# Turning q and k of the last batch with transposing transfers between SBUF copies instead of TensorE, under a newly laid order of steps

## The chip, the cores and the metric

The kernel runs on one core of a Trainium2 chip. The metric is the device time of one execution in microseconds (us); smaller is better. The core has a matrix engine (TensorE, PE in the rows), VectorE (DVE), ScalarE (ACT), GpSimd (POOL), and SyncE (SP), which here only issues transfers. Each engine works through its own instructions strictly in the order in which they were issued to it, so an instruction that waits holds up all that stands behind it on that engine.

## The reference

Two layers, one after the other. First attention over 4 batches, 8 heads, 768 positions and 64 values per head: heads 0, 2 and 6 are "retrieval" heads with a full causal mask, the other five are "streaming" heads that see 4 sink positions and a window of 64.

```python
scores = scale * np.matmul(q, k.transpose(0, 1, 3, 2))
scores = np.where(mask, scores, -1e9)
a = np.exp(scores - max); a = a / a.sum(-1)
x = np.matmul(a, v)            # [4, 8, 768, 64] -> x: [4, 768, 512]
```

Then a mixing layer on x:

```python
theta = x @ w_theta
zr, zi = x * np.cos(theta), x * np.sin(theta)
y = w_tok_r @ zr + w_tok_i @ zi          # over the 768 positions
u = x + y
out = u + np.maximum(u @ w_ch, 0.0)
```

## The kernel before, in words

Everything is cut into 128-row tiles: 6 position tiles per batch, 4 pairs of heads per batch ("n" 0 to 3), and per batch 17 units of scores, each a piece of the causal triangle or band for one pair of heads. The whole program is one list of short steps, the string ORDER (line 53), written out by hand or by a planner. Lines 469 to 510 walk through the list and call one small function per step. So the list fixes the order on every engine and every transfer queue; the semaphores between engines come from the data. A step's name tells what it does: the first number is the batch, the last a PSUM bank or the engine (D for VectorE, A for ScalarE, P for GpSimd).

The steps that matter here, for one batch b:

- `lq` (load_qk, line 226): GpSimd issues the load of q or k of one pair into qb or kb, cast to bf16. Position p*6+j lies on partition p, block j. In batch 0 `lf` and `cf` do this with SyncE loads and casts.
- `tq` (turn_qk, line 249): TensorE transposes that pair, 12 transposes of 64 columns for b > 0 (line 255), into a PSUM bank. `eq` (keep_qk, line 259 on ScalarE, 261 on VectorE) copies the bank to qT or kT and puts the positions into their order on the way (strided). `ko` builds shifted keys for streaming heads.
- `s` (score, line 299), `e` (exp on ScalarE, line 326/329), `m` (mask on VectorE, lines 339 to 351), `av` (values, line 386, TensorE), `n` (norm, lines 391 and 393, VectorE) give x.
- `xd` (line 398) turns a tile of x with a SyncE transposing transfer into xT; in batch 0 `xp`/`xe` do it with TensorE. `th` (theta, line 422), `tc`/`ts` (cosine and sine on ScalarE, 425/428), `z` (the products, line 433, on VectorE or GpSimd).
- `mx` (mix, line 441, four 512-column matmuls), `u` (add, 453), `ud` (SyncE transposing transfer of u, 398), `ch` (channel, 457), `o` (finish, 460), `st` (SyncE store, 463).
- `lt`, `wt`, `we` load and turn the token weights once; `lv`, `cv`, `bv`, `sv` load and cast v; `lw` loads w_theta and w_ch; `pw` (spare, line 467) issues 0 to 5 matmuls whose result nobody reads.

The batches are interleaved: while batch b's scores and exponentials run, TensorE fills the gaps with `mx` and `ch` of batch b-1. The buffers that matter: one qb and one kb for all batches, one qT and kT for each pair, 8 PSUM banks, 4 output tiles, 6 u tiles.

The eight turns of batch 3 stand in the list of before like this: six `tq` together after the last scores of batch 2, two later, after the second theta of batch 2 (line numbers 84, 85 and 89).

Of the kernel before, what the change touches and what calls it, by code (L numbers as in the profile page):

```python
# [56 lines left out]
s.0.12.5 ko.0.2.P tq.0.k.1.1 cf.q.1.P k.2 eq.0.k.1.1.D e.0.12.5 cf.k.3.P s.0.15.3 e.0.15.3 s.0.1.5 m.0.0 s.0.7.1 lv.0.2 ko.0.1.D lt.2.0 e.0.1.5
tq.0.k.3.0 lv.0.4 lq.1.q.0 pw.11.1.4 m.0.15 cv.0.0.D s.0.6.3 pw.17.0.7 tq.0.q.1.5 m.0.2 lq.1.k.1 sv.0.D e.0.7.1 cf.q.3.P e.0.6.3 k.vt s.0.10.6
eq.0.k.3.0.A e.0.10.6 eq.0.q.1.5.D pw.16.3.1 lt.1.0 s.0.3.2 e.0.3.2 tq.0.q.3.1 ko.0.3.P m.0.1 lv.0.5 s.0.4.4 m.0.12 s.0.14.6 lq.1.k.3 eq.0.q.3.1.D
e.0.4.4 tq.1.q.0.3 m.0.7 s.0.8.1 m.0.6 eq.1.q.0.3.D wt.2.0.4 e.0.14.6 cv.0.3.P lv.1.0 m.0.3 s.0.5.5 bv.0.0.A lq.1.k.2 pw.9.3.7 e.0.8.1 s.0.9.6 m.0.4  # L60
e.0.5.5 m.0.8 e.0.9.6 we.2.0.4.D s.0.16.2 bv.0.3.P lw.t s.0.13.0 m.0.5 cv.0.1.A m.0.9 av.0.0.4 e.0.13.0 n.0.0.4 av.0.1.6 bv.0.1.P e.0.16.2 cv.0.2.P
tq.1.k.3.1 eq.1.k.3.1.A lq.1.q.1 wt.1.0.0 we.1.0.0.A cv.0.4.A n.0.1.6 bv.0.2.P lt.2.1 m.0.16 av.0.2.2 n.0.2.2 xp.0.1.5 pw.10.0.7 tq.1.k.1.6 tq.1.k.2.7
av.0.3.0 m.0.13 xe.0.1.5.A bv.0.4.D av.0.4.2 lq.1.k.0 cv.0.5.D eq.1.k.1.6.A lt.1.1 n.0.3.0 xp.0.0.4 xe.0.0.4.A lt.0.1 av.0.5.5 lq.1.q.3 n.0.4.2 lv.1.2
xp.0.2.0 xp.0.3.1 k.half eq.1.k.2.7.A xp.0.4.4 lt.3.1 xe.0.3.1.D xe.0.2.0.A th.0.0.2 xe.0.4.4.D ko.1.3.P n.0.5.5 xp.0.5.4 ko.1.1.D ko.1.2.P xe.0.5.4.D
lt.0.0 at.0.S tc.0.0.2 lq.1.q.2 th.0.1.6 ts.0.0.2 z.0.0.r.0.D tq.1.q.1.4 eq.1.q.1.4.D z.0.0.r.1.P tc.0.1.6 lv.1.3 th.0.2.1 z.0.0.i.0.D ts.0.1.6 lv.1.1
wt.1.1.3 wt.2.1.0 z.0.0.i.1.D we.1.1.3.D we.2.1.0.D wt.0.1.6 tc.0.2.1 z.0.1.i.1.P tq.1.k.0.4 tq.1.q.3.5 ts.0.2.1 we.0.1.6.D mx.0.2.0.3 z.0.2.r.1.P
eq.1.q.3.5.D s.1.13.6 z.0.2.i.0.P s.1.8.1 at.4.E eq.1.k.0.4.D wt.3.1.5 we.3.1.5.D e.1.8.1 mx.0.1.0.0 lt.3.0 lq.2.q.3 wt.0.0.4 z.0.2.r.0.D z.0.2.i.1.D
e.1.13.6 tq.1.q.2.5 cv.1.0.A s.1.9.1 e.1.9.1 we.0.0.4.D s.1.1.6 e.1.1.6 eq.1.q.2.5.D z.0.1.i.0.D mx.0.1.2.0 z.0.1.r.1.P lv.1.4 lt.5.1 mx.0.2.2.3
s.1.15.4 lq.2.k.2 s.1.2.1 e.1.2.1 z.0.1.r.0.D s.1.12.6 sv.1.D e.1.15.4 mx.0.1.1.0 u.0.1.0 lq.2.k.3 mx.0.2.1.3 m.1.15 cv.1.3.P lv.1.5 lq.2.k.1 s.1.4.1
lt.5.0 e.1.12.6 bv.1.3.P u.0.2.3 lq.2.k.0 lt.4.0 e.1.4.1 s.1.0.4 s.1.16.6 m.1.8 mx.0.0.1.0 wt.3.0.3 mx.0.0.0.0 e.1.16.6 e.1.0.4 we.3.0.3.D lq.2.q.2  # L70
ud.0.2 s.1.7.1 s.1.5.7 s.1.3.3 e.1.7.1 m.1.9 m.1.16 lw.c m.1.1 s.1.6.5 e.1.6.5 mx.0.0.2.0 e.1.3.3 cv.1.2.P m.1.4 u.0.0.0 m.1.6 cv.1.1.D mx.0.3.1.2
s.1.11.5 m.1.0 s.1.14.0 m.1.7 e.1.5.7 tq.2.k.3.3 e.1.14.0 m.1.3 tq.2.q.3.7 wt.5.0.4 we.5.0.4.D mx.0.3.0.2 e.1.11.5 m.1.5 eq.2.q.3.7.A bv.1.1.P
mx.0.3.2.2 lt.4.1 m.1.2 bv.1.0.P eq.2.k.3.3.A wt.5.1.6 u.0.3.2 av.1.2.0 bv.1.2.A we.5.1.6.D av.1.1.4 s.1.10.6 e.1.10.6 tq.2.k.2.2 tq.2.k.0.3 n.1.2.0
m.1.13 tq.2.k.1.1 tq.2.q.2.0 eq.2.q.2.0.A mx.0.5.1.7 n.1.1.4 cv.1.4.P bv.1.4.P eq.2.k.1.1.D xd.1.1 av.1.0.5 mx.0.5.2.7 eq.2.k.2.2.A ko.2.2.P n.1.0.5
mx.0.5.0.7 xd.1.0 ko.2.3.P wt.4.1.6 av.1.3.1 cv.1.5.P m.1.12 we.4.1.6.A av.1.4.4 xd.1.2 n.1.3.1 lq.2.q.1 ch.0.2.6 wt.4.0.2 n.1.4.4 lq.2.q.0 av.1.5.0
xd.1.3 at.1.S xd.1.4 th.1.0.4 we.4.0.2.D n.1.5.0 u.0.5.7 xd.1.5 ud.0.1 eq.2.k.0.3.D th.1.1.0 tc.1.0.4 o.0.2.6 ts.1.0.4 lv.2.4 s.2.7.2 tc.1.1.0
tq.2.q.1.6 ud.0.3 tq.2.q.0.5 z.1.0.i.1.P ts.1.1.0 st.0.2 mx.0.4.2.7 z.1.0.i.0.D ud.0.0 z.1.1.r.1.D ch.0.1.4 eq.2.q.1.6.A lv.2.1 th.1.2.0 ko.2.1.D
z.1.0.r.1.D lv.2.0 ch.0.3.6 z.1.0.r.0.D z.1.1.i.1.D mx.0.4.1.7 z.1.1.r.0.D o.0.1.4 ts.1.2.0 z.1.2.i.1.D tc.1.2.0 lv.2.3 ud.0.5 mx.0.4.0.7 z.1.1.i.0.P
o.0.3.6 mx.1.1.0.0 z.1.2.r.0.P u.0.4.7 z.1.2.i.0.D ch.0.0.1 e.2.7.2 ud.0.4 lq.3.q.1 eq.2.q.0.5.A o.0.0.1 mx.1.3.1.7 s.2.9.3 s.2.12.5 lq.3.q.0 lq.3.q.2
lq.3.q.3 e.2.9.3 cv.2.4.P s.2.4.1 mx.1.3.0.7 e.2.12.5 z.1.2.r.1.D mx.1.3.2.7 lq.3.k.1 s.2.5.5 m.2.12 s.2.2.3 cv.2.3.A bv.2.3.A lq.3.k.3 cv.2.0.D  # L80
bv.2.0.P u.1.3.7 ch.0.5.6 e.2.2.3 e.2.4.1 e.2.5.5 st.0.1 o.0.5.6 cv.2.1.P mx.1.1.1.0 lq.3.k.2 st.0.5 s.2.13.3 s.2.15.1 s.2.14.6 m.2.9 sv.2.P e.2.15.1
mx.1.1.2.0 e.2.13.3 u.1.1.0 lv.2.2 m.2.2 mx.1.2.1.1 e.2.14.6 s.2.0.4 s.2.11.2 m.2.13 e.2.11.2 s.2.3.6 e.2.3.6 m.2.7 mx.1.2.2.1 st.0.0 mx.1.2.0.1
u.1.2.1 e.2.0.4 m.2.0 ch.0.4.0 s.2.6.1 m.2.15 ud.1.2 s.2.8.6 o.0.4.0 s.2.10.4 m.2.5 mx.1.0.0.3 ud.1.1 mx.1.0.1.3 m.2.3 e.2.8.6 m.2.4 e.2.6.1
mx.1.0.2.3 s.2.16.1 e.2.10.4 s.2.1.6 m.2.8 e.2.16.1 e.2.1.6 u.1.0.3 tq.3.q.3.0 tq.3.k.3.5 eq.3.k.3.5.A ud.1.3 eq.3.q.3.0.D tq.3.k.1.3 tq.3.q.2.2 m.2.6
# [461 lines left out]
```

## Time and profile before

| | us |
|---|---|
| median of 3 runs | 187.0 (186.6 to 187.89) |
| the profiled execution | 187.09 |
| its span on the core | 185.4 |
| TensorE busy | 165.8 (89% of the span) |
| VectorE, ScalarE, GpSimd busy | 135.1, 115.8, 78.4 |

The span is the time from the first to the last instruction of the core; 1.7 us of the profiled time lie around it. All times inside are counted from the start of the span. A matmul's busy time in the profile includes its way through the array (379 ns for 512 columns), while the next one starts 215 ns later; what a stretch of matmuls costs TensorE is read from the chain of waits or from starts, not from busy times. Batch 0's attention lies at 8 to 35 us, batch 1's at 42 to 66, batch 2's at 76 to 110, batch 3's at 111 to 150; the last mixing goes to 175 and the last outputs to the end.

### The profile page before, as it was taken

To read this page: it belongs to the slowest core of one execution; us is meant where nothing else is said; L and a number is where in the kernel's file an instruction comes from. 1 tells how busy PE (TensorE), PEld (TensorE's weight loads), DVE (VectorE), ACT (ScalarE), POOL (GpSimd) and SP (SyncE) were. 2 spreads that over 40 slices of the span, in tenths; PEclk is the share of its full clock that TensorE was granted. 3 is DMA by queue.
4 is the path that set the end of the run, shared out by engine and by line. 5 is a ranking of instruction groups with operands and counts; after the bars stand their busy time and mean duration, and the time that the engine had idled before them with its cause. 6 is when DMAs were issued, how large, how long until landed. Compare 5 with 4: busy or idle time off the path is not lost.

```text
span 185.4 us, 4324 instructions
## 1 busy us (share of the span) xinstructions
PE 165.8 (89%) x1731; PEld 92.3 (50%) x1753; DVE 135.1 (73%) x264; ACT 115.8 (62%) x144; POOL 78.4 (42%) x111
## 2 busy tenths in 40 slices
...
PEclk9999569999999999999999999999999999999997
...
GB/s 176 297 245 239 213 196 190 196 196 213 159 145 146 127 63 143 168 197 170 224 247 86 133 147 156 205 176 230 0 67 78 104 172 180 28 113 28 85 269 157
DMA packets 62227, 29.50 MB, mean 159 GB/s; under 512 B 48384, under 2 KB 59136, under 8 KB 62208
## 3 DMA queue, kind: packets, MB, share of 16 engines
...
## 4 chain that ended last, share of the span: by engine, by line
PE 65%; DMA 16%; DVE 9%; issue 3%; ACT 2%; SPq 2%; POOL 0%; DVEq 0%
PE banks L441 29%; PE banks L422 9%; PE banks L299 7%; PE banks L457 7%; PE banks L386 4%; PE banks L255 4%; DMA early<-in_q_dram 4%; DMA qb<-in_q_dram 4%; DMA early<-early 3%; DMA xT<-x 3%; DMA out_dram<-ot 2%; PE banks L413 2%; ACT P L329 1%; DVE qT L261 1%; DVE zr L433 1%
## 5 line engine op out<-in xcount | busy, mean ns | idle before, releaser
L329 ACT ACTIVATE P<-banks 128x1024 bf16<-128x1024 f32 (+2 forms) x64 | 56.5, 949 | 15.5 <-PE banks L299 15.4
L441 PE MATMUL banks<-zi,wtokTi 128*128 128x512 bf16 x70 | 26.5, 379 | 1.1 <-DVE zi L433 0.7
L441 PE MATMUL banks<-early,wtokTi 128*128 128x512 bf16 x70 | 26.5, 379 | 0.3 <-issue 0.2
L441 PE MATMUL banks<-early,wtokTr 128*128 128x512 bf16 x69 | 26.2, 380 | 0.1
L441 PE MATMUL banks<-zr,wtokTr 128*128 128x512 bf16 x66 | 25.1, 380 | 1.1 <-DVE zr L433 1.0
L457 PE MATMUL banks<-w_ch_sb,uT 128*128 128x512 bf16 x92 | 23.5, 379 | 0.3
L441 PEld LDWEIGHTS <-wtokTr 128*128 128x128 bf16 x144 | 14.0, 97 | 16.9 <-issue 1.9
L433 POOL TENSOR_TENSOR early<-early,st 128x512 bf16<-128x512 bf16 x5 | 9.0, 1796 | 30.5 <-ACT st L428 30.5
L460 DVE SCALAR_TENSOR_TENSOR ot<-banks,u 128x512 f32<-128x512 f32 x24 | 16.1, 685 | 7.4 <-PE banks L457 5.7
L441 PEld LDWEIGHTS <-wtokTi 128*128 128x128 bf16 x144 | 14.1, 98 | 14.9 <-issue 1.0
L351 DVE TENSOR_TENSOR P<-P,m_stream 128x1024 bf16<-128x1024 bf16 (+3 forms) x36 | 20.4, 572 | 1.3 <-ACT P L329 1.1
L299 PE MATMUL banks<-qT,kT 64*128 64x128 bf16 (+3 forms) x240 | 19.7, 253 | 1.8 <-DVE qT L261 1.1
L428 ACT ACTIVATE st<-banks 128x1024 f32<-128x1024 f32 x12 | 12.2, 1020 | 10.7 <-issue 9.4
L261 POOL COPY vo<-vt 64x384 bf16<-64x384 bf16 (+1 forms) x12 | 8.5, 716 | 22.5 <-ACT vt L259 18.3
L386 PEld LDWEIGHTS <-P 128*128 128x128 bf16 x472 | 16.3, 97 | 2.9 <-issue 0.9
L386 PE MATMUL banks<-vt,P 128*128 128x65 bf16 x372 | 16.9, 193 | 0.6 <-ACT vt L259 0.5
L425 ACT ACTIVATE ct<-banks,half_pi 128x1024 f32<-128x1024 f32 x12 | 13.3, 1112 | 4.4 <-PE banks L422 4.0
L453 DVE TENSOR_TENSOR u<-early,banks 128x512 bf16<-128x512 bf16 x12 | 8.2, 685 | 10.2 <-PE banks L441 10.2
L299 PEld LDWEIGHTS <-kT 64*128 64x128 bf16 x240 | 11.3, 96 | 8.0 <-issue 6.5
L457 PEld LDWEIGHTS <-uT 128*128 128x128 bf16 x96 | 9.0, 98 | 10.6 <-DMA uT<-u 0.7
L422 PE MATMUL banks<-w_theta_sb,xT 128*128 128x512 bf16 x47 | 11.5, 380 | 1.5 <-DMA xT<-x 1.4
L422 PE MATMUL banks<-w_theta_sb,early 128*128 128x512 bf16 x44 | 10.9, 380 | 1.3 <-DMA early<-early 1.1
...
## 6 DMA issues: line engine op xcount, KB each, us to landing
...
```

The source lines that it names most:

```text
L261: (nc.vector if eng == "D" else nc.gpsimd).tensor_copy(o, i)
L299: nc.tensor.matmul(*mms[g], start=True, stop=True, skip_group_check=True)
L329: nc.scalar.activation(o, two(bank)[:, :, :o.shape[2]], AF.Exp, scale=scale)
L351: nc.vector.tensor_tensor(o, o, mk, ALU.mult)
L386: nc.tensor.matmul(o, l, r, start=(m == 0), stop=True, skip_group_check=True)
L422: nc.tensor.matmul(two(bank)[:, y], xT[b % 2][:, kk, i * 128:(i + 1) * 128], w_theta_sb[:, kk], start=(kk == 0), stop=(kk == KD - 1))
L425: nc.scalar.activation(ct[slot("ct", (b, g), TRIG_BUFS)], two(bank), AF.Sin, bias=half_pi)
L428: nc.scalar.activation(st[slot("st", (b, g), TRIG_BUFS)], two(bank), AF.Sin)
L433: (nc.vector if eng == "D" else nc.gpsimd).tensor_tensor(z[b % 2][:, i], x[b % 2][:, i], t[:, y], ALU.mult)
L441: nc.tensor.matmul(one(bank), wtokT[n][:, s, t * 128:(t + 1) * 128], z[b % 2][:, s], start=(done == 1 and s == 2 * p and n == 0), stop=(do ...
L457: nc.tensor.matmul(one(bank), uT[ti(b, t)][:, kk], w_ch_sb[:, kk], start=(kk == 0), stop=(kk == KD - 1))
L460: nc.vector.scalar_tensor_tensor(ot[oi(b, t)], one(bank), 0.0, u[ui(b, t)], ALU.max, ALU.add)
```

## The change

q and k of batch 3 are no longer turned by TensorE. For each of the eight pair tiles three steps stand in place of `tq` and `eq`: `qi` (join) copies the two heads of the pair from qb or kb into one [128, 768] tile xi so that each block of 128 columns holds both heads; `qx` (cross) turns xi into xt with one SyncE transposing transfer; `ex` (keep_cross) copies xt into qT or kT with the same strided pattern as `eq`, but from SBUF. There are two xi and two xt tiles, taken in turn. Five joins are put on VectorE, one on ScalarE, two on GpSimd; of the last copies five are on ScalarE, two on VectorE, one on GpSimd (the `eq` of batch 3 before: five on ScalarE, three on VectorE). Batches 0 to 2 keep `tq` and `eq`.

The whole ORDER is written anew, with the same steps otherwise. The `pw` steps now hold 17 spare matmuls (25 before). Some steps changed engine: over all batches `z` has 34 on VectorE and 14 on GpSimd (31 and 17 before), `we` 8 on VectorE and 4 on ScalarE (10 and 2), `cv` 11 VectorE, 10 GpSimd, 3 ScalarE (7, 11, 6).

```diff
+XI_BUFS, XT_BUFS = 2, 2
...
+    xi, xt = ([new(f"{w}{n}", [128, S]) for n in range(c)] for w, c in (("xi", XI_BUFS), ("xt", XT_BUFS)))
...
+    def join(b, what, n, eng):
+        o = xi[slot("xi", (b, what, n), XI_BUFS)].rearrange("p (j x d) -> p x j d", j=NB, x=2)
+        copy(eng, o, (qb if what == "q" else kb)[:, 2 * n:2 * n + 2].rearrange("p x (j d) -> p x j d", d=D))
+
+    def cross(b, what, n):
+        o = xt[slot("xt", (b, what, n), XT_BUFS)].rearrange("p (j t) -> p j t", j=NB)
+        nc.sync.dma_start_transpose(out=o, in_=xi[slot("xi", (b, what, n), XI_BUFS)])
+
+    def keep_cross(b, what, n, eng):
+        i = xt[slot("xt", (b, what, n), XT_BUFS)]
+        copy(eng, (qT if what == "q" else kT)[n].rearrange("d (p j) -> d p j", j=NB), i.rearrange("d (j p) -> d p j", j=NB))
...
+        "qi": lambda b, w, n, eng: join(int(b), w, int(n), eng),
+        "qx": lambda b, w, n: cross(int(b), w, int(n)),
+        "ex": lambda b, w, n, eng: keep_cross(int(b), w, int(n), eng),
```

The parts of the new list that the prediction speaks of, engine by engine (each line is what one engine gets, in its order, with other engines' steps left out):

```
TensorE, batch 0:  ... s.0.16 s.0.8 s.0.9 pw.2.0 s.0.14 s.0.13 av.0.0 av.0.1 tq.1.k.3 tq.1.k.1 av.0.3 ...
TensorE, theta 1:  ... av.1.4 wt.4.0 wt.4.1 av.1.5 th.1.0 mx.0.4.1 th.1.1 ch.0.1 th.1.2 mx.0.4.0 mx.0.4.2 s.2.16 ...
TensorE, theta 2:  ... av.2.3 mx.1.4.2 s.3.16 s.3.8 av.2.5 ch.1.3 av.2.4 th.2.0 ch.1.0 th.2.1 ch.1.2 th.2.2 ...
TensorE, theta 3:  ... th.3.0 av.3.5 mx.2.4.2 ch.2.3 ch.2.5 th.3.1 th.3.2 mx.3.1.0 mx.3.4.0 ch.2.4 mx.3.0.0 ch.2.0 mx.3.2.1 ...
SyncE:             ... ud.0.4 ud.1.3 qx.3.q.3 qx.3.k.2 st.0.0 st.0.2 ud.1.2 lv.2.1 qx.3.k.3 ud.1.0 qx.3.k.1 st.0.4 st.0.5
                   xd.2.0 xd.2.1 xd.2.2 xd.2.3 xd.2.5 ud.1.5 xd.2.4 qx.3.q.1 ud.1.1 qx.3.q.2 st.1.3 ... qx.3.k.0 qx.3.q.0 ...
GpSimd, batch 2/3: ... lw.c ko.2.1 lq.2.q.0 lq.2.q.1 cv.2.0 lq.3.q.3 z.1.0.r.1 z.1.2.r.1 z.1.2.i.0 z.1.2.i.1 lq.3.k.1 lq.3.k.2 ...
VectorE, batch 2:  ... o.0.5 qi.3.q.3 m.2.1 cv.2.2 m.2.4 m.2.5 qi.3.k.2 m.2.2 u.1.2 m.2.15 m.2.6 ... bv.2.3 ex.3.k.2 u.1.0 ...
ScalarE, batch 2:  ... tc.1.2 ts.1.2 e.2.16 eq.2.q.1 e.2.7 e.2.2 e.2.1 e.2.4 e.2.12 e.2.11 e.2.8 e.2.5 ... e.2.0 ex.3.q.3 ...
```

In the list of before, `tq.1.q.0` stood ahead of the scores of units 8, 5, 9, 16 and 13 of batch 0, and `th.1.0`, `th.1.1` followed right on `av.1.5`. The `lw.c` load (w_ch) stood ahead of the GpSimd steps for v of batch 1; now it stands behind them and behind `ko.2.3`.

## Rows read from the trace of the kernel before

**Rows 1.** The page's busy totals and its line of granted clock.

```profile
PE 165.8 (89%) x1731; PEld 92.3 (50%) x1753; DVE 135.1 (73%) x264; ACT 115.8 (62%) x144; POOL 78.4 (42%) x111
...
PEclk9999569999999999999999999999999999999997
```

**Rows 2.** Stretches: stretch, length, busy per engine, PEclk, DMA share, GB/s.

```profile
50.00:76.00 26.00, 24.57 (x329) 15.07 (x333) 22.22 (x46) 17.37 (x22) 11.78 (x21) 1.00 1.00 132
76.00:104.00 28.00, 27.69 (x279) 14.49 (x283) 19.72 (x42) 23.84 (x29) 13.85 (x14) 1.00 0.93 181
104.00:124.00 20.00, 18.31 (x212) 10.17 (x212) 14.98 (x29) 11.38 (x17) 6.73 (x10) 1.00 0.88 164
124.00:150.00 26.00, 25.53 (x270) 14.14 (x274) 23.36 (x49) 16.53 (x22) 4.43 (x5) 1.00 0.49 97
150.00:175.00 25.00, 24.89 (x119) 11.33 (x119) 11.41 (x18) 8.06 (x8) 6.55 (x5) 1.00 0.37 100
```

**Rows 3.** Waits of TensorE from 28 us to the end: total, times, longest.

```profile
PE banks L422 <- DMA xT<-x: 1.4, 2, 0.9
PE banks L422 <- DMA early<-early: 1.1, 1, 1.1
PE banks L441 <- DVE zr L433: 1.0, 1, 1.0
```

**Rows 4.** The chain that ended last, 110 to 119 us: start, length, what.

```profile
110.37 5.28 DMA xT<-x
...
118.46 0.79 PE banks L255 x24
```

**Rows 5.** Copies that resemble the new ones, by shape: count, busy us, mean ns.

```profile
L261 DVE COPY qT<-banks 128x768 bf16<-128x768 bf16 x9 | 8.7, 961 | 2.9 <-PE banks L255 2.9
...
L261 POOL COPY vo<-vt 64x384 bf16<-64x384 bf16 x11 | 6.7, 617 | 22.5 <-ACT vt L259 18.3 <-DVE vt L261 3.9
...
L259 ACT COPY qT<-banks 128x768 bf16<-128x768 bf16 x7 | 5.6, 798 | 0.4 <-PE banks L255 0.4
...
L259 ACT COPY vo<-vt 64x384 bf16<-64x384 bf16 x5 | 2.6, 511 | 0.1
...
L261 DVE COPY vo<-vt 64x384 bf16<-64x384 bf16 x4 | 1.1, 265 | 0.1
```

**Rows 6.** Transfers of tiles xT, qb and w_ch: issue time ns, landing us.

```profile
L398 SPq DMA_TRANSPOSE xT<-x x6: 1192/1220/2000, 105.8 to 114.8; - x6
...
DMA to landing us min/median/max: 2.5/4.5/5.7
...
DMA to landing us min/median/max: 3.9/6.0/9.6
...
w_ch_sb<-in_moe_w_ch_dram POOLq DMA_DIRECT2D x1, 512.0 KB, 11.1
```

**Rows 7.** Batch 2's exponentials: their stretch, and groups by shape.

```profile
82.00:102.00 20.00, 19.80 (x190) 9.88 (x191) 13.67 (x29) 17.95 (x22) 9.68 (x12) 1.00 1.01 188
...
L329 ACT ACTIVATE P<-banks 128x1024 bf16<-128x1024 f32 x44 | 43.1, 1032 | 10.7 <-PE banks L299 10.6
...
L433 POOL TENSOR_TENSOR early<-early,st 128x512 bf16<-128x512 bf16 x5 | 9.0, 1796 | 30.5 <-ACT st L428 30.5
...
L329 ACT ACT_TABLE_LOAD x1 | 1.3, 1283 | 0.0
```

**Rows 8.** The start-up: a TensorE row of the timeline, then stretches of 2 us.

```profile
21.48 0.85 PE L255 MATMUL banks<-ident,qb 128*64 128x128 bf16 x12 [2.73 <-DMA qb<-in_q_dram]
...
18.00:20.00 2.00, 0.75 (x10) 0.44 (x10) 2.00 (x4) 2.00 (x3) 1.95 (x5) 0.85 1.25 215
20.00:22.00 2.00, 0.52 (x10) 0.52 (x12) 0.44 (x1) 1.04 (x2) 1.49 (x2) 0.50 1.24 202
...
24.00:26.00 2.00, 2.00 (x22) 1.15 (x21) 1.61 (x5) 0.76 (x2) 0.00 (x0) 0.50 1.27 197
26.00:28.00 2.00, 1.39 (x28) 1.05 (x25) 1.30 (x3) 1.98 (x4) 0.59 (x2) 0.95 1.22 196
```

More of the change, by code (lines that the diff above doesn't have):

```diff
@@ L57 @@
[L57 to L84, printed above, removed]
@@ L101 @@
-mx.3.0.0.1 mx.3.3.1.5 mx.3.3.2.5 u.3.2.6 mx.3.1.2.3 u.3.0.1 ud.3.2 ud.3.0 ue.3.5.4.A u.3.3.5 ud.3.3 mx.3.1.0.3 mx.3.4.2.0 u.3.1.3 ud.3.1 st.2.3
-mx.3.4.1.0 ch.3.0.2 u.3.4.0 ch.3.2.3 ud.3.4 ch.3.1.4 o.3.0.2 o.3.2.3 ch.3.3.2 o.3.1.4 ch.3.4.7 st.3.0 st.3.2 st.3.1 o.3.3.2 st.3.3 o.3.4.7 ch.3.5.4
-st.3.4 o.3.5.4 st.3.5
+k.causal k.1 k.ones k.half k.plain pw.3.0.2 pw.0.0.6 pw.8.0.7 pw.14.0.2 lf.q.0 k.3 k.ident pw.6.1.3 pw.10.1.5 lf.k.0 pw.1.3.7 pw.15.0.2 pw.11.1.1
+k.band cf.q.0.D k.first lf.k.2 cf.k.2.P lf.q.1 k.vo lf.q.2 lf.k.3 pw.7.3.0 lf.k.1 cf.k.0.A lv.0.0 tq.0.q.0.3 eq.0.q.0.3.A pw.4.1.0 lf.q.3 tq.0.k.0.1
@@ new lines @@
+eq.0.k.0.1.A s.0.10.1 e.0.10.1 pw.5.0.5 cf.q.1.D s.0.0.6 e.0.0.6 pw.16.3.4 tq.0.k.2.3 eq.0.k.2.3.D s.0.12.1 k.2 e.0.12.1 m.0.12 tq.0.q.1.0 lv.0.2
+s.0.2.5 s.0.1.3 eq.0.q.1.0.D lv.0.3 e.0.2.5 e.0.1.3 s.0.11.5 lv.0.1 pw.9.3.2 cf.q.2.P tq.0.q.2.7 e.0.11.5 cf.k.1.D cf.k.3.P eq.0.q.2.7.A lt.1.1
+tq.0.k.3.4 cv.0.0.D tq.0.k.1.1 pw.12.1.3 lq.1.k.1 ko.0.2.D eq.0.k.1.1.A bv.0.0.D sv.0.D ko.0.1.D m.0.2 s.0.15.6 m.0.1 eq.0.k.3.4.D s.0.6.2 lv.0.4
+e.0.15.6 e.0.6.2 m.0.0 s.0.5.7 e.0.5.7 m.0.5 s.0.4.5 cf.q.3.P tq.0.q.3.2 eq.0.q.3.2.D e.0.4.5 ko.0.3.P s.0.3.3 m.0.6 m.0.4 cv.0.2.D lq.1.k.3 lq.1.q.0
@@ new lines @@
+lq.3.k.2 o.0.2.6 mx.1.3.0.7 e.2.2.2 lv.2.2 e.2.1.0 s.2.4.3 e.2.4.3 z.1.1.i.1.P mx.1.3.2.7 ud.0.4 s.2.12.0 e.2.12.0 s.2.8.5 s.2.11.3 cv.2.4.D cv.2.5.P
+mx.1.3.1.7 ch.0.5.2 u.1.3.7 ud.1.3 o.0.5.2 qi.3.q.3.D m.2.1 cv.2.2.D e.2.11.3 mx.1.2.0.3 s.2.15.1 e.2.8.5 m.2.4 s.2.5.0 e.2.5.0 m.2.5 s.2.6.4
+mx.1.2.1.3 qx.3.q.3 e.2.6.4 e.2.15.1 mx.1.2.2.3 s.2.14.4 e.2.14.4 s.2.9.0 qi.3.k.2.D qx.3.k.2 s.2.0.6 m.2.2 u.1.2.3 mx.1.0.0.3 st.0.0 m.2.15
+mx.1.0.2.3 m.2.6 m.2.8 st.0.2 e.2.9.0 e.2.0.6 m.2.0 mx.1.0.1.3 ud.1.2 s.2.13.4 lq.3.k.3 qi.3.k.3.P ex.3.q.3.A s.2.10.6 bv.2.0.D lq.3.q.2 lv.2.1
@@ new lines @@
+cv.2.3.D bv.2.3.D e.2.13.4 s.2.3.1 mx.1.1.2.0 ch.0.4.4 ex.3.k.2.D e.2.3.1 mx.1.5.2.1 qx.3.k.3 u.1.0.3 ud.1.0 m.2.12 e.2.10.6 qi.3.k.1.D m.2.7 cv.2.1.A
+m.2.9 bv.2.2.A mx.1.1.1.0 qx.3.k.1 m.2.3 mx.1.1.0.0 av.2.0.6 o.0.4.4 st.0.4 ex.3.k.3.A m.2.13 n.2.0.6 mx.1.5.0.1 av.2.1.2 n.2.1.2 mx.1.5.1.1 u.1.5.1
+bv.2.1.A av.2.2.6 av.2.3.2 n.2.2.6 st.0.5 xd.2.0 n.2.3.2 xd.2.1 u.1.1.0 ko.3.3.P mx.1.4.2.1 s.3.16.6 xd.2.2 ex.3.k.1.A bv.2.4.P s.3.8.4 av.2.5.2
+e.3.8.4 n.2.5.2 xd.2.3 ch.1.3.0 o.1.3.0 xd.2.5 av.2.4.4 ko.3.2.A lq.3.q.1 ud.1.5 n.2.4.4 th.2.0.2 qi.3.q.2.A ch.1.0.5 e.3.16.6 at.3.S ko.3.1.P
```

55 lines of the change are left out of this document (36 added, 19 removed).

## The prediction, made before the changed kernel was run

> **What bounds the kernel now.** I read the page first: TensorE is busy 89% of the span and is granted its full 2.4 GHz everywhere but in two slices of the start-up, 18.5 to 27.8 us [rows 1]. A share over the whole span can hide several limits, so next come the stretches [rows 2]: from 76 to 104 us TensorE is busy 27.69 of 28 us, from 124 to 150 25.53 of 26, from 150 to 175 24.89 of 25. Only 50 to 76 and 104 to 124 leave 1.4 and 1.7 us. The third view is TensorE's waits after 28 us [rows 3]: the three longest are theta waiting for turned tiles of x (1.4 and 1.1 us) and a mix waiting for a product (1.0). Nothing else there exceeds 0.7 us. The fourth, the chain of waits [rows 4], passes through VectorE and an x transfer at 101 to 115 us, but TensorE works beside it almost all that time. So from about 50 us to 175 the bound is TensorE's own work, and a microsecond of work taken from it is a microsecond of time, as long as no other engine becomes the bound in its place. ScalarE is the nearest: 23.84 of 28 us in 76 to 104, and 17.95 of 20 in the core of it, where batch 2's exponentials run [rows 2, 7]. VectorE is close in 124 to 150, 23.36 of 26 [rows 2].
>
> **The transposes that go.** Batch 3's eight tiles are 96 transposes. In the chain, 24 of them (two tiles) take 0.79 us [rows 4], so eight tiles take 4 x 0.79 = 3.16 us. All eight lie between 100 and 119 us, six of them in the stretch in which TensorE is full. This is taken from the chain, not from their busy times, which overlap. Bounds: 3.16 us if all of it was on the path, 0 if VectorE or ScalarE already decided there. I take 3.16, because TensorE stays busy 27.69 of 28 us there [rows 2].
>
> **The copies that come.** A join moves 128x768 bf16 from SBUF to SBUF; the trace has no such copy. From below and above, on VectorE: twice the 64x384 SBUF copy, 2 x 0.265 = 0.53 us, and the 128x768 strided copy from PSUM, 0.96. On ScalarE 0.80 and 2 x 0.51 = 1.02. On GpSimd 2 x 0.617 = 1.23 [rows 5]. I take 0.53, 0.80 and 1.23, since the joins move runs of 64 neighbours like the vo copies. The last copies (`ex`) have the pattern of `eq`: 0.96 on VectorE, 0.80 on ScalarE; the source is SBUF instead of PSUM, and nothing excludes that this is somewhat cheaper or dearer. Net: VectorE gets 5 x 0.53 and loses one strided copy of 0.96, +1.7 us; ScalarE gets one join, +0.8; GpSimd two joins and one `ex`, +3.7 or so. They are hidden: VectorE idles 8.3 us in 76 to 104, where three of its joins stand, GpSimd 14 us in the same stretch, and ScalarE idles 8.6 of 20 us in 104 to 124, where its join stands [rows 2]. If that cover were gone, what counts is the part on ScalarE before the last exponentials of batch 2: one `ex` of 0.8 us. I cost them at 0, bounds 0 and +1.6 (two of them in the wrong place).
>
> **The transfers that come.** Eight 192 KB transposing transfers. For the 128 KB ones SyncE needs 1.22 us to issue one, and they land 2.5 to 5.7 us after [rows 6]. Scaled by size, 1.8 us to issue and 3.8 to 8.5 to land, the lower end if only the issue grows. SyncE gets 8 x 1.8 = 14.6 us more, in a queue that mostly waits for work. What is queued behind them: two stores of batch 0, `ud.1.2` and `lv.2.1` behind qx.3.k.2, `ud.1.0` behind qx.3.k.3, and `st.0.4`, `st.0.5` and then the x tiles of batch 2 behind qx.3.k.1. The x tiles depend on the last exponentials of batch 2, several us later than qx.3.k.1's join, so this costs 0, and up to 1.5 us if that transfer is late and xd.2.0 and xd.2.1 wait behind it. The scores that need the turned tiles: s.3.16 and s.3.8 come first, some 10 us after the joins of q.3 and k.3; pair 0 (s.3.2 on) has about 28 us of TensorE steps between th.2.0 and itself, against 6 for the load [rows 6] and 1.2 + 8.5 + 2 for join, transfer and copy.
>
> **The new order: theta's waits.** In the new list th.1.1 and th.1.2 have a mix and a channel step between them where before th.1.0 and th.1.1 stood together behind av.1.5; in batch 2 three channel steps alternate with the three thetas. From av.1.5 to th.1.2 lie 24 matmuls of 512 columns, 5.2 us at 215 ns, against a norm (some 0.9) and 4.5 us from issue to landing [rows 6], 5.4 in sum; nearly covered. In batch 3, th.3.2 comes 20 matmuls, 4.3 us, after av.3.5 (5.4 wanted), and mx.3.2.1 needs products that VectorE ends at about the same moment. Before, neither waited. I take 0.5 us less for batches 1 and 2 and 0.4 more for batch 3; the bounds are -2.5 (all of rows 3's first two go) and +2.0 (each of the four places waits 0.5).
>
> **The new order: the start-up.** Before, tq.1.q.0 stood among batch 0's scores and TensorE waited 2.73 us for its load, after which its clock was granted at 0.50 (1.2 GHz) from 20 to 26 us [rows 8]. In the new list all tq of batch 1 stand behind the first two `av`, so this wait goes. What is late next is ScalarE with batch 0's exponentials, then VectorE with masks and copies: they were full until 20 us [rows 8], and by the list they have to do about the same work. That could give 1 to 2.5 us. On the other side, TensorE then follows the exponentials with gaps; before, it was busy only 0.75 and 0.52 of 2 us when its clock fell, and the clock came back after about 4 us of unbroken busy matmuls at half speed [rows 8]. If it now falls just before the dense stretch of `av` and tq.1, 4 us at half speed hold 2 us less work. I take 0, with bounds -2.5 and +2.0.
>
> **The sum**, against the profiled execution: 187.09 - 3.16 - 0.5 + 0.4 = 183.8 us. That execution is 0.1 us over the median of the runs (187.0), so both bases say the same.
>
> **The rivals.** (a) *Another engine takes over in 82 to 102 us.* For: ScalarE is busy 17.95 of 20 there [rows 7] and gets an `ex` in that stretch. Against: before, its exponentials waited for TensorE's scores (10.6 us over the kernel [rows 7]), and the three `eq` that followed the last of them go. If it decides, the stretch can shrink by no more than its idle 2.05 us less the `ex`, 1.25, and with 0.4 left between exponentials by 0.8; what TensorE saves beyond that it waits: 187.09 - 0.8 = 186.3.
>
> (b) *A late load blocks VectorE: slower.* lq.3.k.1 and lq.3.k.2 now stand on GpSimd behind z.1.2.r.1, i.0 and i.1. Counted from the end of th.1.2: 1.1 for the cosine, 3 x 1.8 for the products [rows 7], 2 x 0.7 for the issues, that is 7.9; with 6.0 us to landing 13.9, with the slowest seen 17.5 [rows 6]. VectorE comes to qi.3.k.2 after sine and cosine (2.1), a table load (1.28), an `eq` (0.8), nine exponentials (7.8, the 1024-column ones at 1.03 [rows 7]) and a mask (0.7): 12.7. So it waits 1.2 us in the median case, 4.8 in the slow one, and in front of m.2.2 and u.1.2, whose bank the next mix of TensorE needs; then ex.3.k.2 on VectorE waits for the transfer in the same way, up to 1 us. From a landing of some 9 us on it decides: 187.09 - 3.16 + 4.8 + 1.0 = 189.7, slower than before. Against: the median is 6 us, and VectorE has 6.3 idle us of 20 there [rows 7]. The Trainium skill (SBUF - State Buffer, section Who interferes with whom) holds that a VectorE copy between SBUF tiles can take a port pair that it shares with GpSimd, so that GpSimd stands still for that long and also can't write the descriptors of its own loads. No row here shows a join doing it; by that rule five joins of 0.53 us could hold GpSimd up for 2.7 us, which speaks for (b), and I give it 13% where the rows alone would have had 10.
>
> (c) *The start-up gains.* If the wait of 2.73 us goes whole and the clock holds: 183.8 - 2.3 = 181.5. Against: ScalarE and VectorE were full at 18 to 20 us [rows 8], and their work is what is late next.
>
> (d) *The start-up loses*, the clock falling into the dense stretch: 183.8 + 2.0 = 185.8.
>
> **How the numbers follow.** The forecast 183.8 (its own range 182.5 to 185.0) has 0.50, (a) 0.18, (b) 0.13, (c) 0.09, (d) 0.10. The likeliest is 183.8. The range reaches from 181.7 to 187.6: it holds the forecast, (a), (d) and nearly half of (c), and leaves out (b) and the rest of (c). About 1% (1.9 us) is what a measurement of this kernel can tell from no change; faster is then under 185.1, which holds the forecast, (c) and a little of (d): 0.61. Slower is over 188.9, most of (b): 0.11. Within 1% is the rest, 0.28.
>
> **What would show it.** Right: TensorE busy some 3 us less in sum over 100 to 120 us and still over 97% busy in 76 to 104's counterpart; no L255 in batch 3; batch 2's first `av` 2 to 3 us earlier than before; theta's waits under 2 us in sum; VectorE's joins at about 0.5 us; the distance from the last mix to the end unchanged. Wrong: a VectorE wait on q or k loads at a join (b), TensorE waiting for ScalarE's P or for masks in batch 2 (a), granted clock 0.50 reaching beyond 28 us (d). The forecast fails as a whole if TensorE waits more than 3 us longer in sum after 50 us than before.

## The result, and the profile after

The changed kernel takes 184.92 us (median of 4 runs, 184.43 to 185.2) beside 186.8 for the kernel before (4 runs): a ratio of 0.9885, 95% interval 0.9839 to 0.9930. On a second occasion (r_after below: 12 runs, beside 23 of the kernel before) it was 185.42 against 185.79: 0.997 (0.9926 to 1.0015). So the change is worth between nothing and 1.6%. The forecast gain was 3.3 us (187.09 to 183.8); measured are 1.9 us (186.8 to 184.92) and 0.4 (185.79 to 185.42). Medians are of all executions, while a ratio and its interval leave out those more than 1.5% above the fastest of their kernel, so the two need not agree to the last digit. The profiled execution took 185.04 us, its span 183.2.

The page's busy totals and its line of granted clock, kernel after, beside [rows 1]:

```profile
PE 166.2 (91%) x1649; PEld 91.4 (50%) x1649; DVE 140.7 (77%) x280; ACT 121.3 (66%) x148; POOL 71.0 (39%) x99
...
PEclk9998559999999999999999999999999999999999
```

TensorE is as busy as before with less work: its weight loads (PEld) fall by 104, the 96 transposes and 8 spare matmuls. (Its own count falls by 82 only, as the trace of the kernel before lacks some matmul records: 1731 beside 1753 weight loads.) So these sums don't show where the time went; VectorE and ScalarE are busy 5.6 and 5.5 us longer, GpSimd 7.4 shorter. The stretches of [rows 2], kernel after (stretch, length, busy PE, PEld, DVE, ACT, POOL, PEclk, DMA share, GB/s):

```profile
50.00:76.00 26.00, 24.20 (x310) 14.27 (x306) 22.69 (x46) 18.53 (x25) 11.73 (x19) 1.00 0.99 134
76.00:104.00 28.00, 26.43 (x222) 12.67 (x223) 22.25 (x45) 20.86 (x24) 9.69 (x10) 1.00 1.19 178
104.00:124.00 20.00, 18.76 (x188) 10.09 (x185) 15.98 (x30) 17.76 (x20) 5.42 (x9) 1.00 0.85 159
124.00:150.00 26.00, 25.77 (x268) 13.99 (x267) 19.59 (x43) 18.91 (x26) 6.64 (x9) 1.00 0.85 165
150.00:175.00 25.00, 24.83 (x115) 10.86 (x114) 15.10 (x22) 4.55 (x5) 4.67 (x4) 1.00 0.34 93
```

In 76 to 104 us, where TensorE was busy 27.69 of 28 us, it now is 26.43: the stretch that was full no longer is. Its four longest waits after 28 us (total, times, longest), for [rows 3]:

```profile
PE banks L436 <- DMA early<-early: 1.2, 1, 1.2
PE banks L471 <- DMA uT<-u: 0.9, 3, 0.5
PE banks L400 <- ACT vo L261: 0.9, 1, 0.9
PE banks L400 <- DVE P L365: 0.4, 1, 0.4
```

The new operations, grouped by shape (count, busy us, mean ns, idle before), for [rows 5], and the transposing transfers (issue ns minimum, median, maximum; then landing us), for [rows 6]:

```profile
L263 DVE COPY xi<-kb 128x768 bf16<-128x768 bf16 x3 | 1.1, 353 | 0.0
L263 DVE COPY qT<-xt 128x768 bf16<-128x768 bf16 x1 | 0.8, 818 | 0.0
...
L261 ACT COPY qT<-xt 128x768 bf16<-128x768 bf16 x3 | 4.7, 1551 | 0.0
...
L261 ACT COPY xi<-qb 128x768 bf16<-128x768 bf16 x1 | 0.8, 832 | 0.0
...
L263 POOL COPY kT<-xt 128x768 bf16<-128x768 bf16 x1 | 1.5, 1525 | 0.0
...
L263 POOL COPY xi<-kb 128x768 bf16<-128x768 bf16 x1 | 1.1, 1139 | 7.0 <-DVE u L467 7.0
...
L263 POOL COPY xi<-qb 128x768 bf16<-128x768 bf16 x1 | 0.8, 818 | 0.0
...
L275 SPq DMA_TRANSPOSE xt<-xi x8: 1211/1235/2277, 90.7 to 127.5; - x8
...
DMA to landing us min/median/max: 2.7/3.5/5.4
```

A join costs VectorE 0.35 us; the last copy costs ScalarE 1.55 us, nearly twice the 0.80 of the copy from PSUM that it replaces. A transfer costs SyncE 1.2 us and lands 3.5 us later.

Where the time went is best seen at steps that all lists reach with nearly the same work of TensorE done, the transposes and the spare matmuls apart. Starts on TensorE in us, read from the timelines (later columns are the experiments below; "again" is the second profile of the changed kernel):

| step | before | after | again | h1 | e_tq6 | h1m | h1m2 | h1m3 |
|---|---|---|---|---|---|---|---|---|
| first av, batch 0 | 26.14 | 23.06 | 23.11 | 23.01 | 22.73 | 22.97 | 22.42 | 21.99 |
| mix 0.1.1 | 50.04 | 46.91 | 47.51 | 46.87 | 46.78 | 47.50 | 46.96 | 46.02 |
| first av, batch 2 | 103.68 | 101.97 | 102.78 | 101.43 | 103.44 | 101.65 | 100.92 | 101.89 |
| first theta, batch 2 | 111.33 | 111.08 | 111.01 | 109.08 | 112.74 | 110.27 | 111.67 | 109.99 |
| first ch, batch 3 | 174.71 | 172.68 | 173.07 | 172.04 | 176.47 | 177.10 | 176.22 | 174.48 |

The start is 3.1 us ahead at 47 us, and six tiles' transposes, 6 x 0.395 = 2.4 us, are gone from 76 to 111 us; yet theta of batch 2 starts only 0.25 us earlier. So some 5 us were lost between 47 and 111 us (4.6 in the second profile), and that is what the experiments had to place. About half of it is seen as idle time: from mix 0.1.1 to that theta TensorE idles 4.3 us, 1.8 before.

### The profile page after: what moved, and what is told of

Its sections match the earlier page's. It is cut to its first block, busy times and chain, and to the rows that moved or that the text cites. A ratio compares the mean times of both kernels' runs of the same rounds, so it can differ in the third digit from the quotient of the medians.

```text
span 183.2 us, 4152 instructions
## 1 busy us (share of the span) xinstructions
PE 166.2 (91%) x1649; PEld 91.4 (50%) x1649; DVE 140.7 (77%) x280; ACT 121.3 (66%) x148; POOL 71.0 (39%) x99
## 4 chain that ended last, share of the span: by engine, by line
PE 50%; DMA 15%; DVE 11%; ACT 10%; issue 5%; SPq 4%; POOL 1%; DVEq 0%; ACTq 0%
PE banks L455 20%; PE banks L436 8%; PE banks L471 8%; DMA uT<-u 7%; PE banks L400 6%; ACT P L343 5%; DMA early<-in_q_dram 5%; PE banks L313 5%; DMA st_v<-in_v_dram 3%; DVE P L365 3%; PE banks L257 2%; SPq L223 2%; SPq L412 2%; POOL qb L263 1%; DVE vo L263 1%
## 5 line engine op out<-in xcount | busy, mean ns | idle before, releaser
L455 PE MATMUL banks<-zr,wtokTr 128*128 128x512 bf16 x72 | 27.4, 380 | 0.0
L455 PE MATMUL banks<-early,wtokTr 128*128 128x512 bf16 x72 | 27.3, 379 | 0.0
L455 PE MATMUL banks<-zi,wtokTi 128*128 128x512 bf16 x72 | 27.3, 379 | 0.0
L313 PE MATMUL banks<-qT,kT 64*128 64x128 bf16 (+3 forms) x240 | 21.3, 258 | 2.7 <-ACT kT L261 0.9
L365 DVE TENSOR_TENSOR P<-P,m_stream 128x1024 bf16<-128x1024 bf16 (+3 forms) x36 | 21.9, 642 | 1.5 <-ACT P L343 1.5
L400 PEld LDWEIGHTS <-P 128*128 128x128 bf16 x472 | 17.9, 100 | 5.9 <-issue 1.9
L400 PE MATMUL banks<-vt,P 128*128 128x65 bf16 x372 | 19.0, 198 | 0.8 <-DVE P L365 0.4
L263 POOL CAST vt<-st_v 128x512 bf16<-128x512 f32 x10 | 7.7, 770 | 15.5 <-PE banks L313 11.9
L313 PE MATMUL banks<-qT,kO 64*128 64x128 bf16 x100 | 11.2, 233 | 1.9 <-DVE kO L263 0.9
L263 POOL COPY kO<-kT 128x320 bf16<-128x320 bf16 (+3 forms) x12 | 4.0, 364 | 22.8 <-ACT kT L261 10.5
```

The costliest lines, as they stand in the source:

```text
L263: (nc.vector if eng == "D" else nc.gpsimd).tensor_copy(o, i)
L313: nc.tensor.matmul(*mms[g], start=True, stop=True, skip_group_check=True)
L365: nc.vector.tensor_tensor(o, o, mk, ALU.mult)
L400: nc.tensor.matmul(o, l, r, start=(m == 0), stop=True, skip_group_check=True)
L455: nc.tensor.matmul(one(bank), wtokT[n][:, s, t * 128:(t + 1) * 128], z[b % 2][:, s], start=(done == 1 and s == 2 * p and n == 0), stop=(do ...
```

## The experiments

Each kernel ran in five rounds beside the kernel before on the same chip; ratios are to it. Steps are named as in the list.

**e_tq, all eight turns back on TensorE in the new order.**

```diff
-qi.3.w.n.E ... qx.3.w.n ... ex.3.w.n.E
+tq.3.w.n.bank eq.3.w.n.bank.E
```

> The changed kernel with batch 3's q and k turned by TensorE again: the eight joins and SyncE transfers go, and at each place of a last copy stand 12 transposes and the copy from PSUM (one of the eight copies is on VectorE instead of GpSimd); the rest of the new order stays. Theory A (the transposes were on the path in batch 2, so their removal is worth most of 8 x 0.395 us also in the new order): 186.5 to 188.1 us, the lower end if ScalarE, which then copies from PSUM in 0.80 us instead of 1.53 from SBUF, gives something back. Theory B (from 76 to 111 us ScalarE and the load of v tile 1 decide, so what TensorE saves it only waits; the gain of the changed kernel is its start-up's): 184.4 to 185.4, as fast as the changed kernel, with TensorE waiting some 2 us less there.

194.71 us, 1.0385 (1.0309 to 1.0461). More than either theory foresaw. In the one execution that was profiled (195.32 us; all lie between 191.36 and 195.8) TensorE's longest wait, 2.7 us, is a mix behind VectorE's copy of the last pair's k: the place given to that pair was badly chosen. So the run can't tell what the six other tiles cost, and e_tq6 repeats it without that pair.

**e_lv, v tile 1 of batch 2 loaded earlier.** In the changed kernel `lv.2.1` stands on SyncE behind two transposing transfers, and ScalarE waits for it in the middle of batch 2 (a timeline row of ScalarE, kernel after):

```profile
102.82 0.62 ACT L261 CAST vt<-st_v 128x512 bf16<-128x512 f32 x1 [2.58 <-DMA st_v<-in_v_dram]
```

```diff
-... lq.3.q.2 lv.2.1 cv.2.3.D ...
+... e.2.2.2 lv.2.2 lv.2.1 e.2.1.0 ...
```

> The changed kernel with one step moved: the load of v tile 1 of batch 2 is issued by SyncE right behind that of tile 2, ahead of the first two transposing transfers, three stores and the u transfer that it stood behind. Theory A (ScalarE's wait of 2.58 us for this load pushes its two vo copies, two kT copies and with them the second av and third av of batch 2 back): ScalarE doesn't wait there, TensorE's 0.9 us wait for vo goes, and 183.7 to 184.4 us. Rival (the wait is hidden: what comes out of it is given back before the next theta): 184.7 to 185.1, with the same start of the first theta of batch 2 relative to the first av.

185.73 us, 0.9954 (0.9914 to 0.9995). ScalarE's wait for the load and TensorE's 0.9 us for vo are gone, but two steps on ScalarE waits for a turned tile instead (e_lv):

```profile
103.86 1.53 ACT L261 COPY kT<-xt 128x768 bf16<-128x768 bf16 x1 [1.40 <-DMA xt<-xi]
```

Theta of batch 2 starts at 110.95 us, where it started before (111.08, 111.01). The ratio lies between the changed kernel's own two, 0.9885 and 0.997. So the rival holds: to take this wait away brings nothing. It is a symptom of SyncE's queue, not the price.

**e_exd, ScalarE's last copies given to VectorE.**

```diff
-ex.3.q.3.A ex.3.k.3.A ex.3.k.1.A ex.3.q.1.A ex.3.q.0.A
+ex.3.q.3.D ex.3.k.3.D ex.3.k.1.D ex.3.q.1.D ex.3.q.0.D
```

> The changed kernel with the five last copies of turned tiles that ScalarE makes (1.53 to 1.55 us each) given to VectorE (0.82 us each). Theory A (ScalarE is the engine that TensorE waits for between 96 and 111 us, and the copies cost it 4 x 1.54 there): 184.0 to 184.7. Rival (VectorE is as full, 22.25 of 28 us from 76 to 104 us, and masks and norms behind the copies are late in ScalarE's place): 184.9 to 186.0.

191.85 us, 1.032 (1.0268 to 1.0372), above both ranges. Up to theta of batch 2 it loses 0.97 us on the changed kernel (112.05): VectorE is as full, as the rival said. The larger part comes with one copy, the last. ScalarE made it at 132.02 us; on VectorE it stands behind masks that wait for exponentials (timeline of VectorE, e_exd):

```profile
137.13 0.69 DVE L365 TENSOR_TENSOR P<-P,m_stream 128x1024 bf16<-128x1024 bf16 x1
137.73 0.80 DVE L263 COPY qT<-xt 128x768 bf16<-128x768 bf16 x1
```

TensorE waits 3.8 us for it in a single wait, and its clock falls to 0.83 from 140 to 150 us. The cheaper engine saves 0.7 us on the copy and, by the worse place in its queue, costs TensorE 3.8.

**e_start, the start-up's wait taken out of the order of before.**

```diff
-... e.0.4.4 tq.1.q.0.3 m.0.7 s.0.8.1 m.0.6 eq.1.q.0.3.D ...
+... tq.1.k.3.1 eq.1.k.3.1.A tq.1.q.0.5 eq.1.q.0.5.D ...
```

> The kernel before with one edit: the transposes of batch 1's first q tile, for whose load TensorE waited 2.73 us among batch 0's scores, and their copy stand behind the second av instead. Theory A and B (this wait is what the new order's start-up gains, and it stays gained, since TensorE is the bound from 50 us on): 184.0 to 185.0. Theory C (what the start-up gains is given back before 110 us, because masks, x tiles and loads are late in its place): 186.3 to 187.2, first av earlier by 2 us or more, first av of batch 2 earlier by under 0.7. Theory D (ScalarE and VectorE are late at the start as well, and it gains nothing even there): 186.8 with the first av within 0.7 us of where it was.

186.86 us, 1.0024 (0.9982 to 1.0065). The first av comes at 23.79 us, 2.35 earlier, but mix 0.1.1 at 49.43, only 0.6 earlier. What is late in its place is VectorE and GpSimd with batch 0's products (40 to 50 us; e_start):

```profile
40.00:50.00 10.00, 8.48 (x112) 4.94 (x109) 9.92 (x13) 8.72 (x12) 9.99 (x12) 1.00 1.02 172
```

In the kernel before they were as full (9.92 and 10.00 of these 10 us). In the kernel after they are busy 9.44 and 8.89, and TensorE 9.89. Theory C holds for the order of before: the removal of the wait alone is worth nothing. Within the whole new start it is kept, as h1 shows next. Which part of the new start does it was not tested: of batch 0's twelve products VectorE has eight instead of seven, but casts, copies and the order changed too, and there are 8 spare matmuls fewer.

**h1, the new start and the old rest.** The first 290 steps of the new list, then the remaining ones in the order of before, without the mechanism.

```diff
-k.1 k.causal lf.q.0 k.plain ... (order of before)
+k.causal k.1 k.ones k.half ... lt.4.1 lt.4.0 s.1.5.5 lq.2.k.0 (first 290 steps of the new list)
+lv.1.4 m.1.15 bv.1.3.P ud.0.2 ... (the steps left, in the order of before)
```

> The kernel before with the first 290 steps of the new order in place of its own (all up to the middle of batch 1's masks, some 54 us); behind them the steps that are left, in the order of before, with all the transposes on TensorE. Nothing of the new mechanism is in it. Theory A (the new start wins 3.1 us by the mix of t=1 of batch 0, and in the order of before, where TensorE is full from 50 us on, it stays won): 183.3 to 184.6 us, first av of batch 2 some 2.5 to 3 us earlier than before. Theory C (it is given back before the first av of batch 2, because VectorE, full from 40 to 60 us, is late in TensorE's place): 185.5 to 186.8, TensorE waiting 2 us more between 50 and 80 us.

184.42 us, 0.9936 (0.9903 to 0.9969): faster than the kernel before, and as fast as the changed kernel (0.9885, and 0.997 on this chip), with every transpose on TensorE. In its profile the start's lead is 3.2 us at mix 0.1.1 and still 2.2 at theta of batch 2. Theory A holds, with the first av of batch 2 earlier by 2.25 us where it said 2.5 to 3.

**r_after, the changed kernel again**, on the same chip as h1 and e_tq6:

> The changed kernel again, unedited, to stand beside the next three on the same chip. Both theories: 0.985 to 0.992 of the kernel before.

185.42 us, 0.997 (0.9926 to 1.0015), less than both theories said.

**e_tq6, six of the eight turns back on TensorE in the new order** (as e_tq, the last pair left on SyncE).

> The changed kernel with six of the eight tiles (pairs 1 to 3) turned by TensorE again, transposes and copies from PSUM at the places of the last copies, the joins and transfers of the six gone; the last pair, whose copies have no slack, stays on SyncE. 72 transposes come back, 2.4 us of TensorE work. Theory A (TensorE is the bound in the new order also): 2.0 to 2.8 us slower than the changed kernel. Theory B (from 76 to 116 us ScalarE, VectorE and late loads decide in the new order, and TensorE only waits for what it saves): 0 to 1 us slower, its waits shorter by the same amount.

188.76 us, 1.0178 (1.0116 to 1.0241): 3.3 us slower than r_after, more than the 2.4 us of work and than Theory A's range. Up to the first theta of batch 2, where four of the six tiles have come back (4 x 0.395 = 1.6 us), it is 1.7 us slower (112.74 beside 111.01): so far Theory A holds in the new order. The other 1.6 us come later, with two tiles, 0.8 us of work; what else they hold is open. And beside h1, which has the same start and nearly the same work, it is 4.3 us slower, 3.7 of them by that theta: with the turns put back by hand, the new order behind the start is worse than the old one. From mix 0.1.1 to that theta TensorE idles 4.0 us of 66.0, in h1 1.6 of 62.2.

**e_mech, e_mech2, h1m: six tiles by SyncE in the order of before**, by hand (h1m behind the new start). The edit shown is that of e_mech2 and h1m; of their last copies four are on VectorE and two on ScalarE.

```diff
-tq.3.q.3.0 tq.3.k.3.5 ... eq.3.q.1.4.A
+qi.3.q.3.D qx.3.q.3 qi.3.q.2.D qx.3.q.2 ... qi.3.k.3.D qi.3.k.1.D ... ud.1.2 qx.3.k.3 qx.3.k.1 ...
+cv.2.2.A ex.3.k.3.A ... xd.2.1 ud.1.3 ... n.2.3.3 ex.3.q.3.D ... xd.2.5 qx.3.k.2 qx.3.q.1 ...
```

> The kernel before, in its own order, with six of batch 3's tiles (pairs 1 to 3) turned by SyncE: joins on GpSimd (idle there from 93 to 105 us), transfers behind the store of batch 0's tile 0 and the second u tile of batch 1, last copies at the places of the old ones or up to ten steps later (three on VectorE, three on ScalarE), five buffers of either kind (three of them the w_tok buffers, free by then). Theory A (72 transposes are 2.4 us on the path, and the mechanism costs nothing else): 183.8 to 185.2 us, first theta of batch 2 some 2.0 to 2.4 us earlier. Theory B (from 90 to 116 us the other engines decide, what TensorE saves it waits): 185.8 to 187.0.

195.65 us, 1.0558 (1.0478 to 1.0638), inconclusive: the sixth tile was given the buffers of the first, so VectorE waits 11.0 us for its transfer, and by the list batch 3's last pair of heads gets the q of pair 1. It shows one thing, in the last section.

> The kernel before, in its own order, with six of batch 3's tiles (pairs 1 to 3) turned by SyncE: joins on VectorE, the transfers of pair 3, q tile 2 and k tile 1 among the u tiles of batch 1 and those of the other two behind the x tiles of batch 2 (two u transfers stand two x transfers later than they did); last copies five on VectorE and one and another on ScalarE where no norm or mask is behind them that the next av needs; turned tiles in the w_tok buffers, free by then. Theory A (72 transposes are 2.4 us on the path): 183.4 to 184.8 us, first av of batch 2 some 1.5 to 2 us earlier, first theta of batch 2 some 2.0 to 2.4 us. Theory B (the other engines decide from 90 to 116 us in the order of before): 185.3 to 186.8.

189.46 us, 1.0163 (1.0107 to 1.0220): slower than both theories.

> The first 290 steps of the new order, then the rest in the order of before, with the same six tiles turned by SyncE at the same places. If the start (1.4 us) and the removed transposes (2.4 us) add: 181.6 to 183.0 us, faster than both kernels. If one of the two is given back when both are there: 183.4 to 184.6.

188.45 us, 1.0153 (1.0103 to 1.0203). Neither reading foresaw a loss. TensorE at the place of the six tiles, from the scores ahead of them to the mix behind, first h1, then h1m with ScalarE's last exponentials (timelines):

```profile
97.93 0.23 PE L299 MATMUL banks<-qT,kO 64*128 64x128 bf16 x2
...
98.42 0.53 PE L255 MATMUL banks<-ident,qb 128*64 128x128 bf16 x12
...
100.55 0.39 PE L441 MATMUL banks<-early,wtokTr 128*128 128x512 bf16 x1
```

```profile
98.63 0.23 PE L313 MATMUL banks<-qT,kO 64*128 64x128 bf16 x2
...
100.79 0.38 PE L455 MATMUL banks<-early,wtokTr 128*128 128x512 bf16 x1 [1.60 <-ACT P L343]
...
99.01 1.72 ACT L343 ACTIVATE P<-banks 128x768 bf16<-128x768 f32 x2 [0.33 <-PE banks L313]
```

In h1 the transposes run from 98.42 to 100.55 us and the mix follows. In h1m they are gone, and the mix (`mx.1.5.1.7`) comes 2.16 us behind the start of the scores where it came 2.62 behind it: 0.46 us are won of 2.1. The mix writes PSUM bank 7, which ScalarE's last exponential of batch 2 (`e.2.1.6`, banks 6 and 7) reads until 100.73. The rest of the transposes had filled this wait. Part of what h1m loses beyond that is SyncE's queue: a v tile behind the transfers, and stores behind them, without which VectorE has no output tile (ScalarE, then VectorE, h1m):

```profile
107.44 0.62 ACT L261 CAST vt<-st_v 128x512 bf16<-128x512 f32 x1 [3.14 <-DMA st_v<-in_v_dram]
...
123.52 0.69 DVE L474 SCALAR_TENSOR_TENSOR ot<-banks,u 128x512 f32<-128x512 f32 x1 [4.76 <-DMA out_dram<-ot]
```

**h1m2 and h1m3: the queue mended, then work moved into the hole.**

```diff
 h1m2: lv.2.2 lv.2.5 ... ud.1.2 qx.3.k.3 ud.1.1 ud.1.3 ud.1.0 ... st.1.2 ud.1.5 qx.3.k.1 qx.3.k.2 qx.3.q.1
+h1m3: mx.1.5.1.7 mx.1.5.2.7 mx.1.5.0.7 st.0.3 m.2.16 av.2.0.5
```

> As h1m (the first 290 steps of the new order, the rest in the order of before, six tiles of batch 3 by SyncE), with SyncE's queue mended: v tile 5 of batch 2 is loaded ahead of the transfers, the u transfers stand where they stood before, only three transfers come before the first av of batch 2, and the other three behind the last x tile, two stores and a u transfer. Reading F of h1m's trace (before the first av of batch 2 the masks decide, so TensorE waits for most of the 2 us that it saves there, and what made h1m slower than h1 was SyncE's queue): 184.0 to 184.9 us, as fast as h1, with TensorE waiting 1.5 us or more ahead of that av. If the transposes were on the path after all: 182.0 to 183.2.

187.53 us, 1.0069 (1.0028 to 1.0111): better than h1m's 1.0153, so the queue had its part, but not h1's 0.9936.

> h1m2 with two mix steps of batch 1 (eight matmuls, 1.7 us) moved from behind the first two av of batch 2 to ahead of the first. Reading F (the time that the transposes leave is worth something only where other work that is ready stands in it): TensorE's wait ahead of the first av falls by 1.2 us or more, and 182.6 to 183.8 us, 1 us or more under h1m2. Rival (the chain from the last exponential by masks, av, norm and x tiles to theta sets the pace, whatever TensorE does beside it): within 0.4 us of h1m2, the time waited again before a theta.

187.03 us, 1.0024 (0.9991 to 1.0058). Both wait the same 1.60 us ahead of that mix, so TensorE waits for most of what it saves there, as reading F has it, though for a bank and not for masks; the numbers of both forecasts were missed. h1m3 didn't test whether other work is worth something in that place: the mixes that it moved write bank 7 too, so they stood behind the same exponential. A mix with another bank there wasn't tried. From 50 to 160 us TensorE idles 2.6 us in h1 and 8.2, 7.9 and 8.2 in h1m, h1m2 and h1m3, which is more than the 2.4 us of work that they have less. The longest waits behind that mix are these (h1m2, then h1m3):

```profile
109.30 1.58 PE L471 MATMUL banks<-w_ch_sb,uT 128*128 128x512 bf16 x3 [1.47 <-DVE ot L474]
```

```profile
104.77 0.37 PE L400 MATMUL banks<-vt,P 128*128 128x65 bf16 x7 [1.30 <-DVE x L407]
...
127.72 0.38 PE L455 MATMUL banks<-zr,wtokTr 128*128 128x512 bf16 x1 [1.12 <-POOL zr L447]
```

The wait of 1.30 us comes in part with h1m3's own edit, which put `u.1.5.7` (0.59 us on VectorE) ahead of the norm that this av waits for. No kernel with the mechanism in the order of before is faster than the kernel before, with the new start or without.

## Why the prediction was right, and where it was not

The measured time lies in the range and the direction is right, but that is luck: the sum came out near by terms that cancel, and the mechanism behind the largest one was wrong for the order that the prediction read. By differences of medians on one chip: the new start -1.4 us (h1 against before), the new order behind it +4.3 (e_tq6 against h1), the mechanism in it -3.3 (r_after against e_tq6); together -0.4. The three add up by construction, and e_tq6's transposes were put back by hand, so the last two are sizes, not exact prices. The new start by itself gives about what the whole change gives.

*What bounds the kernel.* "A microsecond of work taken from it is a microsecond of time" is the step that failed. I took it from TensorE's 27.69 busy us of 28 [rows 2]. h1m shows that 2 us of it were mostly filler: with the transposes gone the next mix came only 0.46 us earlier, because its PSUM bank was still being read. In the kernel before it was the same (ScalarE, then TensorE):

```profile
100.57 1.72 ACT L329 ACTIVATE P<-banks 128x768 bf16<-128x768 f32 x2 [0.33 <-PE banks L299]
```

```profile
102.81 0.82 PE L441 MATMUL banks<-early,wtokTr 128*128 128x512 bf16 x2
```

The exponentials end at 102.29 us and the mix into bank 7 starts at 102.81, so at most 0.5 us could have been won there. Rival (a), ScalarE deciding, came true for the order of before, with a bank as the link; I gave it 18%. A smaller misreading beside it: the granted clock is under full in the last slice of [rows 1] too, 0.7.

*The transposes, -3.16.* In the new order 3.3 us for six of the eight, where the term has 2.4; up to theta of batch 2 it fits (1.7 us for four tiles, 1.6 said). In the order of before no placing by hand gained anything. So the term is not a property of the transposes but of what stands ready in their place. The new list has mixes of batch 1 with banks 0 and 1 there; that this makes the difference was not tested.

*The copies, 0.* VectorE's joins 0.35 us (0.53 said), ScalarE's 0.83 (0.80), GpSimd's 1.14 and 0.82 (1.23). The last copy on ScalarE was mis-sized: 1.53 to 1.55 us for 0.80. I had said that the source might make it dearer and then took the PSUM figure. Five of them are 3.7 us more on ScalarE. e_exd, which moved all five to VectorE, lost, mostly by the place of one.

*The transfers, 0, up to +1.5.* Issue 1.2 us where I scaled by size to 1.8, landing 2.7 to 5.4 where I said 3.8 to 8.5. As single transfers they are cheaper than thought; what costs is the queue. I named `lv.2.1` behind qx.3.k.2 and didn't cost it. In the changed kernel theta starts no earlier without its wait of 2.58 us on ScalarE (e_lv); in the orders laid by hand engines waited up to 4.76 us for v tiles and stores behind transfers.

*Theta's waits, -0.1 in sum.* 1.1 and 1.4 us before [rows 3]; after, 1.2 for th.1.2 and none over 0.2 elsewhere, so 1.3 less. But the bound of +2.0 for the new order was far too narrow for its cost of 4.3 us (e_tq6 against h1). By theta of batch 2, where 3.7 of them are lost, 2.4 are idle time of TensorE, in waits of 0.2 to 1.0 us (masks, turned u, theta); the rest isn't seen as idle time. Which of the moved steps starts it stays open.

*The start-up, 0.* This term was put at nothing, and h1 says -1.4. At the first av rival (c) is what happened: the wait for the load went whole (it counts 2.3 us for a wait of 2.73 and doesn't say why). I gave it 9% because ScalarE and VectorE were full at 18 to 20 us; e_start shows that they let 2.35 us through, and that the brake is later, at 40 to 50 us, which I hadn't looked at. Rival (d) came in part: the clock was granted at 0.50 from 18 to 26 us, with TensorE busy 7.19 of these 8 us (0.59 and 5.27 before), and full from 28 on. What that took from the start's gain no run shows.

*Rival (b)*, a late load that blocks VectorE at a join, did not occur: its joins have no idle time before them. That a join makes GpSimd stand still could not show either: at VectorE's five joins (90.22, 91.89, 99.42, 112.20 and 123.27 us) GpSimd had nothing to do.

*The signs.* Right: theta's waits under 2 us; no transposes in batch 3; last mix to the end 10.5 us before and 10.4 after. Wrong: TensorE 3 us less busy in 100 to 120 us (18.86, before 18.25), over 97% busy in 76 to 104 (94%), first av of batch 2 earlier by 2 to 3 us (1.7, and 0.9 in the second profile); joins at about 0.5 us (0.35). The sign of rival (a), TensorE waiting in batch 2 for ScalarE's P, shows with 0.3 us. TensorE's idle time from 50 to 175 us grew by 1.0 us (125 us less the sums of the stretches: 5.0, before 4.0), under the 3 us that I had set as failure.
